# Cached attention decode with a squared-ReLU gate: the start and the end of the work sent through the loop's value product

## The chip, the core and the metric

The kernel runs on one core of a Trainium2 chip. TensorE (PE) multiplies, VectorE (DVE), ScalarE (ACT) and GpSimd (POOL) do the work between products, SyncE (SP) issues the transfers (DMAs) from the memory of the chip into the core's SBUF. Sixteen DMA engines carry them. The metric is the time of one execution on the device in microseconds (us), median of several runs.

## What is computed

```python
xn = layernorm(x)                                  # x: 2 x 1 x 512
q = (xn @ wq) -> 2 x 32 heads x 1 x 128            # wq: 512 x 4096
p = softmax(q . k_cache * 128 ** -0.5)             # k_cache: 2 x 8 x 32768 x 128, four q heads share one
o = p . v_cache                                    # v_cache: 2 x 8 x 32768 x 128
s = o @ wo                                         # wo: 4096 x 512
h = relu(xn @ w1 + b1) ** 2                        # w1: 512 x 1792
out = x + s * silu(h @ w2 + b2)                    # w2: 1792 x 512
```

All is float32. The two caches are 537 MB of the 561 MB that are read.

## The kernel before, in words

**Streams and steps.** The caches are 16 streams (8 key-value heads, 2 batch rows), each cut into two halves, so the loop has 32 steps. A step needs one block of keys (8 MB, tile `kslot`) and one of values (8 MB, tile `vslot`), of which there is one buffer each. The step's scores are 32 products into `sc` (L319). VectorE takes their maximum (L265), a transpose through TensorE and a second reduction make it one per head (L269, L273), ScalarE takes the exponential (L278), TensorE turns the result (L325), ScalarE copies it to `pT` (L280). Then 32 products of 16 x 512 multiply `pT` with `vslot` into `o_ps` (L305): this is the **value product**. ScalarE copies `o_ps` (L228), TensorE turns it (`ot`, L310), VectorE sums its blocks (L243), and once in two steps GpSimd weighs the two halves into `oT` (L248 to L252).

**What sets the order.** TensorE's program is a loop of two blocks, `pe_values` and `pe_scores`, that waits on semaphores against a counter; its start and its end are two more blocks, `pe_first` and `pe_last`, recorded by the class `Later`. The other engines' programs are written out for all 32 steps. SP's queue is in program order: the gate's weights `wm` (into `wbuf`), `wq` (into `vslot`), the first keys; then for each step the values as soon as the value product before has left `vslot` (wait at L255), and the next keys as soon as the scores have left `kslot` (L259); at the end, with no wait of their own, `wo` in six pieces of 16, 8, 4, 2, 1 and 1 heads into `wbuf` (L335), which has been free since the gate. All of these share one queue, so a transfer starts when those issued ahead of it are through.

**Start.** ScalarE's queue loads x, b1 and b2 as small rows. The layernorm (L147 to L173) runs on all 128 partitions with two small products of `ones`. The gate is computed by products of its own into the PSUM tile `wb`: 16 for w1 (L185), 14 for w2 (L200), 4 to gather them (L206). In round 0 of the loop the value product multiplies xn (spread over `pT` at L177) with `wq` in `vslot`: this gives q.

**End.** After the last value product and its weighing, `pe_last` multiplies the heads of `oT` with `wo` as the pieces come: 28 heads into `wb` (L348), the last 4 and the gathered sum of the 28 into `acc` (L354, L359). Then VectorE multiplies with the gate and adds x (L370, L372), and the output goes out (L374).

Of the kernel before, what the change touches and what calls it, by code (L numbers as in the profile page):

```python
# [22 lines left out]
FG = F // NG  # L23
FJ = FG // 32
# [3 lines left out]
PIECES = (16, 8, 4, 2, 1, 1)  # L28
WIDE = 28
SCALE = 1.0 / math.sqrt(DH)  # L30
# [20 lines left out]
class Later:  # L51


    def __init__(self, engine):
        self.engine, self.calls = engine, []

    def __call__(self, f, *a, **k):
        self.calls.append([f, a, k, False])

    def wait(self, *tokens):  # L60
        for token in tokens:
            self(self.engine.wait, token)

    def done(self):
        self.calls[-1][3] = True
        self.engine.n += 1
        return self.engine.sem, self.engine.n

    def emit(self):
        self.engine.seen = {}  # L70
        for f, a, k, last in self.calls:
            ins = f(*a, **k)  # L72
            if last:
                ins.then_inc(self.engine.sem, 1)


def build(nc, x32, x16, kt, vt, wq, wm, wo, out):
# [3 lines left out]
    PE = [mybir.EngineType.PE]  # L81
# [39 lines left out]
    t_one = pool.done(g.memset(ones[:, :], 1.0))  # L121
    t_xT = pool.done(g.memset(xT[:, :], 0.0))
    g.memset(selq[:, :], 0.0)
    t_pT = pool.done(g.memset(pT[:, :], 0.0))
    t_qz = pool.done(g.memset(qz[:, :], 0.0))
    t_oT = pool.done(g.memset(oT[:, :, :], 0.0))
    t_o0 = dve.done(nc.vector.memset(o_ps[:, :], 0.0))

    act.wait(t_xb)
    for lo, hi in ((0, 15), (15, 28), (28, 32)):  # L130
        nc.scalar.dma_start(small[lo:hi, :], x32[lo:hi]).then_inc(small_sem, 16)
    for lo, hi in ((0, 14), (14, 16)):
# [7 lines left out]
    v.tensor_reduce(selg[:, :], ident[:, :].rearrange("p (g y) -> p y g", g=NG), axis=AX.X, op=ALU.add)  # L140
    dve.wait(t_qz)
    t_sel = dve.done(v.tensor_reduce(selq[:, 0:32:16], ident[:, :].rearrange("p (g y) -> p y g", g=NG)[:, 0:2], axis=AX.X, op=ALU.add))


    first = Later(pe)
    first.wait(t_id, (small_sem, 48))
    first(tr, ms[:, 0:32], small[0:32, :], ident[0:32, 0:32])  # L147
    dve.wait(first.done())
    t = dve.done(v.tensor_copy(xs[:, :], ms[:, 0:22]))
    first.wait(t, t_one)  # L150
    first(mm, ms[:, 32:40], ones[:, :], xs[:, 0:8], start=True, stop=True)
    dve.wait(first.done())
    t = dve.done(v.tensor_reduce(st[:, 0:2], ms[:, 32:40].rearrange("p (d b) -> p b d", b=B), axis=AX.X, op=ALU.add))
    dve.wait(t)
    t = dve.done(v.tensor_scalar(st[:, 2:4], st[:, 0:2], -1.0 / D, None, op0=ALU.mult))
    dve.wait(t)
    t = dve.done(v.tensor_tensor(xc[:, :].rearrange("p (d b) -> p d b", b=B), xs[:, 0:8].rearrange("p (d b) -> p d b", b=B),
                                 st[:, None, 2:4].to_broadcast([P, ND, B]), op=ALU.add))
    dve.wait(t)
    t = dve.done(v.tensor_mul(sq[:, :], xc[:, :], xc[:, :]))  # L160
    first.wait(t)
    first(mm, ms[:, 64:72], ones[:, :], sq[:, :], start=True, stop=True)
    dve.wait(first.done())
    t = dve.done(v.tensor_reduce(st[:, 4:6], ms[:, 64:72].rearrange("p (d b) -> p b d", b=B), axis=AX.X, op=ALU.add))
    dve.wait(t)
    t = dve.done(v.tensor_scalar(st[:, 6:8], st[:, 4:6], 1.0 / D, 1e-5, op0=ALU.mult, op1=ALU.add))
    act.wait(t)
    t = act.done(nc.scalar.activation(st[:, 8:10], st[:, 6:8], AF.Sqrt))
    dve.wait(t)
    t = dve.done(v.reciprocal(st[:, 10:12], st[:, 8:10]))  # L170
    dve.wait(t, t_xT)
    t_x = dve.done(v.tensor_tensor(xT[:, :, 0:B], xc[:, :].rearrange("p (d b) -> p d b", b=B),
                                   st[:, None, 10:12].to_broadcast([P, ND, B]), op=ALU.mult))  # L173
    dve.wait(t_x, t_pT)
    pq = pT[:, :].rearrange("p (d f y h) -> p d f y h", d=ND, f=2, h=REP)
    for f in range(2):
        ins = v.tensor_copy(pq[:, :, f, :, 2 * f:2 * f + 2], xT[:, :, None, 0:B].to_broadcast([P, ND, 16, B]))  # L177
    ins.then_inc(gv, 1)


    first.wait(t_x, (wm_sem, 16))
    for d in range(ND):
        for c in range(NG):
            lo = d * F + c * FG
            first(mm, wb[32 * c:32 * c + 32, :FG], xT[:, d, :], wbuf[:, lo:lo + FG], start=(d == 0), stop=(d == ND - 1))  # L185
    dve.wait(first.done())
    t = dve.done(v.tensor_copy(o_sb[:, :FG], wb[:, :FG]))
    dve.wait(t)
    t = dve.done(v.transpose(hT[:, :, :].rearrange("p j b -> p (j b)"), o_sb[:, :FG]))
    dve.wait(t)  # L190
    t = dve.done(v.tensor_tensor(hT[:, :, 0:B], hT[:, :, 0:B], xs[:, 8:22, None].to_broadcast([P, FJ, B]), op=ALU.add))
    dve.wait(t)
    t = dve.done(v.tensor_scalar(hT[:, :, 0:B], hT[:, :, 0:B], 0.0, None, op0=ALU.max))
    dve.wait(t)
    t = dve.done(v.tensor_mul(hT[:, :, 0:B], hT[:, :, 0:B], hT[:, :, 0:B]))
    first.wait(t)
    for j in range(FJ):
# [24 lines left out]
    q_token = [None]
    t_rl = t_add = t_dx = t_wl = t_wr = None
    t_t4 = {}
    for i in range(NT + 1):
        s, u = divmod(i, 2)
        act.wait(at(VD, i))
        nc.scalar.copy(o_sb[:, :], o_ps[:, :]).then_inc(os, 1)  # L228
        if i and not u:

            dve.wait(t_lt)
            t_rl = dve.done(v.reciprocal(rl[:, :], lt[:, :]))
        dve.wait(at(OT, i))
# [19 lines left out]
        if i == NT:  # L253
            break
# [11 lines left out]
        if t_dx and not u:  # L266
            dve.wait(t_dx)
# [151 lines left out]
```

## Time and profile before

| | |
|---|---|
| time, median of 3 runs | 1303.61 us (1303.28 to 1303.71) |
| the profiled execution's own time | 1303.31 us |
| its span, from the first to the last instruction | 1302.0 us |
| TensorE busy | 53% |
| DMA queue of SP | 561.06 MB, 99.7% of 16 engines' span |
| granted TensorE clock, mean | 0.739 |

How to read it: the span is what the rows describe, and the time of an execution is 1.31 us more than its span. A DMA row gives the time from issue to landing, so it includes the time spent behind earlier transfers. A row of the timeline gives start, duration, engine, line, operation, the number of instructions merged, and in brackets how long the engine had been idle and for whom. "PE ... x64" is one value product: a float32 product is two instructions.

### The profile page before, as it was taken

How to read it: one execution, taken by the hardware profiler on the slowest of the kernel's cores; microseconds unless marked ns; L12 is line 12 of the kernel's file. 1: busy time of each engine (PE TensorE's matmuls, PEld its weight loads, DVE VectorE, ACT ScalarE, POOL GpSimd, SP SyncE). 2: the span in 40 equal slices, each digit the busy share in tenths (PEclk: the TensorE clock that was granted, in tenths of full speed). 3: DMA queues.
4: the chain of work that ended last, by engine and by line, in shares of the span. 5: the costliest groups of instructions: out<-in, count | busy, mean ns of one | idle time of the engine just before them, and what ended most of it. 6: DMA issues, size and time to landing. Idle time of an engine off the chain costs nothing.

```text
span 1302.0 us, 10280 instructions
## 1 busy us (share of the span) xinstructions
PE 690.4 (53%) x4685; PEld 191.6 (15%) x4685; DVE 54.2 (4%) x186; ACT 72.3 (6%) x184; POOL 34.9 (3%) x174
## 2 busy tenths in 40 slices
PE   3446446546546545645645654644654554554556
PEld 1111111111111111111111111111111111111111
DVE  1000000000000000000000000000000000000000
ACT  0100000000000000000000000000000000000000
POOL 0000000000000000000000000000000000000000
PEclk9777677677677768667767767767767867777778
DMA  9999999999999999999999999999999999999998
GB/s 418 421 449 421 449 421 445 423 445 425 429 441 421 447 423 445 425 441 429 439 429 427 443 421 447 423 445 425 443 427 439 429 439 431 421 447 423 443 427 357
DMA packets 10617, 561.18 MB, mean 431 GB/s; under 512 B 1216, under 2 KB 1392, under 8 KB 1776
## 3 DMA queue, kind: packets, MB, share of 16 engines
q1 hardware_dynamic: 10512, 561.06, 99.7%
q8 instruction: 2, 0.03, 0.0%
q14 instruction: 7, 0.06, 0.0%
q10 hardware_dynamic: 96, 0.03, 0.0%
HBM read 561.02 MB, written 0.07 MB: 431 GB/s over the span
## 4 chain that ended last, share of the span: by engine, by line
DMA 76%; PE 23%; issue 0%; SPq 0%; DVE 0%
DMA vslot<-in_vt 70%; PE o_ps L305 23%; DMA wbuf<-in_wo 4%; DMA vslot<-in_wq 3%; PE acc L72 0%; SPq L335 0%; SPq L104 0%; SPq L256 0%; DVE yb L370 0%; DVE xb L372 0%; SPq L105 0%
## 5 line engine op out<-in xcount | busy, mean ns | idle before, releaser
L319 PE MATMUL sc<-kslot,qz 128*32 128x512 f32 x2048 | 298.9, 749 | 277.8 <-DMA kslot<-in_kt 277.8
L305 PE MATMUL o_ps<-vslot,pT 128*16 128x512 f32 x2112 | 307.2, 747 | 203.7 <-DMA vslot<-in_vt 196.5
L319 PEld LDWEIGHTS sc<-kslot,qz 128*32 128x32 f32 x2048 | 72.1, 134 | 483.1 <-DMA kslot<-in_kt 285.4
L305 PEld LDWEIGHTS o_ps<-vslot,pT 128*16 128x16 f32 x2112 | 64.4, 114 | 419.2 <-issue 212.4
L278 ACT ACTIVATE prob<-sc,nm 128x512 f32<-128x512 f32 x32 | 22.0, 687 | 661.7 <-DVE nm L273 661.7
L325 PE MATMUL tp<-ident,prob 128*128 128x128 f32 x128 | 28.3, 360 | 53.5 <-ACT prob L278 53.5
L228 ACT COPY o_sb<-o_ps 128x512 f32<-128x512 f32 x33 | 19.3, 586 | 494.1 <-PE o_ps L305 494.1
L265 DVE TENSOR_REDUCE r<-sc 128x1 f32<-128x512 f32 x32 | 22.1, 692 | 570.7 <-PE sc L319 570.7
L310 PE MATMUL ot<-ident,o_sb 128*128 128x128 f32 x132 | 21.7, 287 | 23.6 <-ACT o_sb L228 23.6
L243 DVE TENSOR_REDUCE t<-ot 128x4 f32<-128x64 f32 x32 | 7.2, 225 | 547.7 <-PE ot L310 547.7
L263 POOL COPY qz<-qT 128x4 f32<-128x4 f32 x31 | 5.8, 188 | 833.3 <-PE sc L319 833.3
L325 PEld LDWEIGHTS tp<-ident,prob 128*128 128x128 f32 x128 | 18.1, 178 | 59.6 <-ACT prob L278 59.6
L322 PE MATMUL ms<-ident,r 128*128 128x128 f32 x32 | 10.3, 323 | 26.4 <-DVE r L265 26.4
L310 PEld LDWEIGHTS ot<-ident,o_sb 128*128 128x128 f32 x132 | 13.9, 141 | 54.0 <-ACT o_sb L228 54.0
L280 ACT COPY pT<-tp 128x512 f32<-128x512 f32 x32 | 18.8, 586 | 31.2 <-PE tp L325 31.2
L327 PEld LDWEIGHTS ms<-selh,l 128*128 128x128 f32 x64 | 13.6, 263 | 0.0
L322 PEld LDWEIGHTS ms<-ident,r 128*128 128x128 f32 x32 | 4.2, 133 | 55.4 <-DVE r L265 55.4
L327 PE MATMUL ms<-selh,l 128*128 128x4 f32 x64 | 11.4, 248 | 0.0
L72 PE MATMUL ms<-ident,small 32*128 32x32 f32 x1 | 0.3, 283 | 18.2 <-DMA small<-in_x 18.2
L269 DVE TENSOR_REDUCE mh<-ms 128x4 f32<-128x128 f32 x32 | 9.3, 292 | 13.3 <-PE ms L322 13.3
L250 POOL TENSOR_TENSOR tw<-t,wr 128x8 f32<-128x8 f32 x16 | 3.2, 203 | 247.9 <-DVE t L243 247.9
L271 POOL TENSOR_TENSOR mm<-mh,selm 128x4 f32<-128x4 f32 x32 | 6.5, 203 | 77.1 <-DVE mh L269 77.1
(74 smaller groups left out, 82.0 us busy)
## 6 DMA issues: line engine op xcount, KB each, us to landing
wbuf<-in_wm SPq DMA_DIRECT2D x1, 7168.0 KB, 20.7
wbuf<-in_wo SPq DMA_DIRECT2D x1, 4096.0 KB, 39.3
wbuf<-in_wo SPq DMA_DIRECT2D x1, 2048.0 KB, 43.7
wbuf<-in_wo SPq DMA_DIRECT2D x1, 1024.0 KB, 46.1
kslot<-in_kt SPq DMA_DIRECT2D x32, 29.2
vslot<-in_vt SPq DMA_DIRECT2D x32, 29.3
wbuf<-in_wo SPq DMA_DIRECT2D x1, 512.0 KB, 46.8
wbuf<-in_wo SPq DMA_DIRECT2D x2, 256.0 KB, 47.1
```

The lines of the kernel that those rows point to most:

```text
L228: nc.scalar.copy(o_sb[:, :], o_ps[:, :]).then_inc(os, 1)
L243: t_t4 = dve.done(v.tensor_reduce(t4[:, 1 - u, :], ot[:, :].rearrange("p (i y e) -> p e i y", i=4, y=NG)[:, :REP], axis=AX.XY, op=ALU.add))
L265: v.tensor_reduce(r1[:, :], sc[:, :], axis=AX.X, op=ALU.max).then_inc(dm, 1)
L269: t_mh = dve.done(v.tensor_reduce(mh[:, u, :], ms[:, :P].rearrange("p (a h) -> p h a", h=REP), axis=AX.X, op=ALU.max))
L278: nc.scalar.activation(prob[:, :], sc[:, :], AF.Exp, bias=nm[:, u:u + 1], scale=SCALE, accum_out=l1[:, :]).then_inc(ex, 1)
L280: nc.scalar.copy(pT[:, :], tp[:, :]).then_inc(gv, 1)
L305: ins = mm(o_ps[32 * y:32 * y + 16, :], pT[:, 16 * n:16 * n + 16], vslot[:, n * W:(n + 1) * W], start=(n < NG), stop=(n >= 32 - NG))
L310: ins = tr(ot[:, lo:lo + P], o_sb[:, n * DH:(n + 1) * DH], ident[:, :])
L319: ins = mm(sc[32 * c:32 * c + 32, :], qz[:, 28 - 4 * j:60 - 4 * j], kslot[:, lo:lo + W], start=(j == 0), stop=(j == NJ - 1))
L322: tr(ms[:, :P], r1[:, :].to_broadcast([P, P]), ident[:, :]).then_inc(pe.sem, 1)
L325: ins = tr(tp[:, k * P:(k + 1) * P], prob[:, k * P:(k + 1) * P], ident[:, :])
L327: mm(ms[:, :REP], l1[:, :].to_broadcast([P, P]), selh[:, :], start=True, stop=True).then_inc(pe.sem, 1)
```

## The change

- **Gate through the value product.** `wm` goes into `vslot`, packed on the host to blocks of 512 columns, w1 in blocks 0 to 15 with two of w2's at 11 and 15, the rest of w2 in blocks 16 to 27. `wq` goes into `wbuf`. PE has no blocks of its own for the start: `pe_values` runs three rounds (`PRO = 3`) before the first scores. Round 0 multiplies xn with w1, round 1 the squared ReLU with w2 (both read `vslot` as it is). Then ACT, POOL and DVE copy `wq` from `wbuf` to `vslot` (5700, 5884 and 4800 columns of each partition), and round 2 gives q. The first values are issued after round 2.
- **Layernorm** on two partitions of 512 elements, VectorE alone, with x, b1 and b2 in one load of 8 rows (`xr`), issued after POOL's first instruction; a 32 x 32 transpose and four copies lay the rows out over the partitions (`xs`).
- **End through the value product.** The last values come in two halves on two semaphores (`gv`, `gb`). A value product now waits at blocks 16, 24 and 28 too (`gb`, `gc`, `gd`), and counts `vh` after block 15. When the last values' first half is multiplied, SP issues 12 heads of `wo` into that half of `vslot`; when the second half is, 8, 4 and 4 heads more, then the last 4 heads one by one into `wbuf`. A 36th round multiplies the 28 heads in `vslot` with `pT` (filled from `oS`, L379); the last 4 heads and the gathering are as before.
- **Loops.** VectorE's and ScalarE's programs are loops of 16 rounds (one stream each) with waits against registers; what POOL did in the steps (the key queries `qz`, the maximum's scaling, the weighing) is VectorE's. `Later` and PSUM tile `wb` go.

The diff's core (the host's packing, declarations and the waits of VectorE's loop, which repeat, left out):

```diff
-PIECES = (16, 8, 4, 2, 1, 1)
+PRO = 3
+PIECES = (12, 8, 4, 4)
+TAIL = (1, 1, 1, 1)
...
-    nc.sync.dma_start(wbuf[:, 0:2 * FJ * D], wm).then_inc(wm_sem, 16)
-    nc.sync.dma_start(vslot[:, :], wq).then_inc(gv, 16)
+    nc.sync.dma_start(vslot[:, 0:WM], wm).then_inc(gv, 16)
+    nc.sync.dma_start(wbuf[:, :], wq).then_inc(wq_sem, 16)
     nc.sync.dma_start(kslot[:, :], kt[0, 0]).then_inc(gs, 16)
...
+    o_copy(pro(VD, 0))
+    pool.wait(pro(VD, 0))
+    t_z = pool.done(g.memset(pT[:, :], 0.0))
+    dve.wait(pro(OT, 0))
...
+    for lo, hi, at in ((0, 2, slice(11, 16, 4)), (2, NF, slice(16, 28))):
+        ins = v.tensor_copy(hT[:, at, :, 0:B], hv[:, lo:hi, None, :].to_broadcast([P, hi - lo, 4, B]))
+    ins.then_inc(gv, 17)
+
+    o_copy(pro(VD, 1))
+    pool.wait(pro(VD, 1))
+    t_z = pool.done(g.memset(pT[:, :], 0.0))
+    cuts = (0, 4800, 10500, SLOT)
+    act.wait((wq_sem, 16))
+    t_c0 = act.done(nc.scalar.copy(vslot[:, cuts[1]:cuts[2]], wbuf[:, cuts[1]:cuts[2]]))
+    pool.wait((wq_sem, 16))
+    t_c1 = pool.done(g.tensor_copy(vslot[:, cuts[2]:cuts[3]], wbuf[:, cuts[2]:cuts[3]]))
+    dve.wait(pro(VD, 1), (wq_sem, 16))
+    t_c2 = dve.done(v.tensor_copy(vslot[:, cuts[0]:cuts[1]], wbuf[:, cuts[0]:cuts[1]]))
...
+    dve.wait(t_c0, t_c1, t_c2, t_f)
+    v.tensor_copy(st[:, 6:7], selh[:, 0:1]).then_inc(gv, 17)
...
+    sp.wait(pro(VD, 2))
+    nc.sync.dma_start(vslot[:, :], vt[0, 0]).then_inc(gv, 16)
...
+    with nc.body("sp_last", valid_engines=SP):
+        sp.wait((vh, NT + PRO))
+        h = 0
+        for n, sem in zip(PIECES, (gv, gb, gc, gd)):
+            if h:
+                sp.wait(at(VD, NT - 1))
+            nc.sync.dma_start(vslot[:, (TOP + h) * D:(TOP + h + n) * D], wo[h * P:(h + n) * P].rearrange("(p h) e -> p (h e)", h=n)).then_inc(sem, 16)
+            h += n
+        for n, sem in zip(TAIL, tail_sem):
+            nc.sync.dma_start(wbuf[:, (h - WIDE) * D:(h - WIDE + n) * D], wo[h * P:(h + n) * P].rearrange("(p h) e -> p (h e)", h=n)).then_inc(sem, 16)
...
+    with nc.body("pe_values", valid_engines=PE):
+        i = nc.snap(it, min_val=0, max_val=NT + PRO)
+        w(gv, i * 17 + 17)
+        for n in range(32):
+            if n in (16, 24, 28):
+                w({16: gb, 24: gc, 28: gd}[n], i * 16 + 1)
             y = n % NG
             ins = mm(o_ps[32 * y:32 * y + 16, :], pT[:, 16 * n:16 * n + 16], vslot[:, n * W:(n + 1) * W], start=(n < NG), stop=(n >= 32 - NG))
+            if n == 15:
+                ins.then_inc(vh, 1)
         ins.then_inc(pe.sem, 1)
+        nc.br_lt(it, NT + PRO, on_true="pe_turn", on_false="end", engines=PE)
```

SP's queue at the end, in the kernel before, from the last keys on (`vt` are the values, `kt` the keys; a name in brackets is what the instruction waits for):

```order
L260 DMA kslot<-in_kt 128x16384 [waits pe]
L256 DMA vslot<-in_vt 128x16384 [waits pe]
L335 DMA wbuf<-in_wo 128x8192
L335 DMA wbuf<-in_wo 128x4096
L335 DMA wbuf<-in_wo 128x2048
L335 DMA wbuf<-in_wo 128x1024
L335 DMA wbuf<-in_wo 128x512 x2
```

and in the change:

```order
L237 DMA kslot<-in_kt 128x16384 [waits pe]
L242 DMA vslot<-in_vt 128x8192 [waits pe]
L243 DMA vslot<-in_vt 128x8192
L244 UNCONDITIONAL_BRANCH
L325 DMA vslot<-in_wo 128x6144 [waits vh]
L325 DMA vslot<-in_wo 128x4096 [waits pe]
L325 DMA vslot<-in_wo 128x2048 x2
L328 DMA wbuf<-in_wo 128x512 x4
```

Before, all of `wo` stands behind the last values without a wait; now two waits on TensorE stand between the last values and `wo`.

VectorE's queue in the change between the gate's second product and the first keys' query (in the kernel before `wq` lands in `vslot` itself and nothing stands here but the gate's own steps):

```order
L201 COPY vslot<-wbuf 128x4800 [waits wq,pe]
L203 TENSOR_REDUCE y<-ot 128x8 [waits pe]
L207 COPY pT<-xs 128x4x16x2 [waits pool]
L207 COPY pT<-xs 128x4x16x2
L209 TENSOR_TENSOR y<-y,xs 128x8 [waits dve]
L211 COPY st<-selh 128x1 [waits pool,dve,act]
L223 COPY qT<-ot 128x4x4x2 [waits pe]
```

The copy at L211 is the one that lets TensorE start round 2: it waits for the three copies of `wq`.

## Rows read from the trace of the kernel before

**Rows 1.** The page: SP's DMA queue (packets, MB, share), and the chain.
```profile
q1 hardware_dynamic: 10512, 561.06, 99.7%
...
DMA vslot<-in_vt 70%; PE o_ps L305 23%; DMA wbuf<-in_wo 4%; DMA vslot<-in_wq 3%; PE acc L72 0%; SPq L335 0%; SPq L104 0%; SPq L256 0%; DVE yb L370 0%; DVE xb L372 0%; SPq L105 0%
```

**Rows 2.** Timeline of the start (start us, duration us, engine, what, idle before).
```profile
18.17 0.28 PE L72 MATMUL ms<-ident,small 32*128 32x32 f32 x1 [18.17 <-DMA small<-in_x]
...
28.87 3.63 PE L72 MATMUL wb<-wbuf,hT 128*32 128x512 f32 x28 [2.10 <-DVE hT L195]
...
40.82 9.50 PE L305 MATMUL o_ps<-vslot,pT 128*16 128x512 f32 x64 [7.22 <-DMA vslot<-in_wq]
...
50.40 0.33 SPq L256 DMA_DIRECT2D vslot<-in_vt  x1
50.41 0.59 ACT L228 COPY o_sb<-o_ps 128x512 f32<-128x512 f32 x1 [15.66 <-PE o_ps L305]
...
51.74 0.31 DVE L237 COPY qT<-ot 128x32 f32<-128x32 f32 x2 [16.67 <-PE ot L310]
...
60.17 8.38 PE L319 MATMUL sc<-kslot,qz 128*32 128x512 f32 x64 [8.47 <-DMA kslot<-in_kt]
```

**Rows 3.** The chain in order of time: the first values' transfer, the fastest and the slowest product.
```profile
50.40 29.08 DMA vslot<-in_vt
...
118.23 8.41 PE o_ps L305 x64
...
234.34 10.08 PE o_ps L305 x64
```

**Rows 4.** DMA issues: KB each, us from issue to landing.
```profile
wbuf<-in_wm SPq DMA_DIRECT2D x1, 7168.0 KB, 20.7
...
wbuf<-in_wo SPq DMA_DIRECT2D x2, 256.0 KB, 47.1
out<-xb SPq DMA_DIRECT2D x1, 64.0 KB, 1.5
```

**Rows 5.** DMA queues, packets between 6 and 9.5 us (packets, MB, share).
```profile
q10 hardware_dynamic: 29, 0.01, 0.9%
```

**Rows 6.** Groups of instructions, shapes apart (count, busy us, mean ns).
```profile
L284 ACT COPY lh<-ms 128x4 f32<-128x4 f32 x32 | 5.4, 168 | 0.0
L187 DVE COPY o_sb<-wb 128x448 f32<-128x448 f32 x1 | 0.6, 625 | 4.6 <-PE wb L72 4.6
L126 POOL MEMSET oT<- 128x1024 f32 x1 | 1.0, 954 | 0.0
L124 POOL MEMSET pT<- 128x512 f32 x1 | 0.5, 528 | 0.0
L177 DVE COPY pT<-xT 128x128 f32<-128x128 f32 x2 | 0.4, 224 | 0.0
L155 DVE TENSOR_SCALAR st<-st 128x2 f32<-128x2 f32 x1 | 0.2, 169 | 0.0
```

**Rows 7.** Waits: who waited for whom, us in total, times, longest.
```profile
DVE r L265 <- PE sc L319: 570.7, 32, 18.4
```

**Rows 8.** Timeline of the end.
```profile
1249.70 2.80 SPq L335 DMA_DIRECT2D wbuf<-in_wo  x6
...
1272.69 0.59 ACT L280 COPY pT<-tp 128x512 f32<-128x512 f32 x1 [0.74 <-PE tp L325]
...
1279.29 9.79 PE L305 MATMUL o_ps<-vslot,pT 128*16 128x512 f32 x64 [6.52 <-DMA vslot<-in_vt]
...
1291.14 0.20 POOL L252 TENSOR_TENSOR oT<-tw 128x4 f32<-128x4 f32 x1
...
1299.27 0.43 PE L72 MATMUL acc<-wbuf,oT 128*32 128x128 f32 x8
```

**Rows 9.** Two stretches near the end (length, busy of each engine, granted clock, DMA).
```profile
1264.40:1274.60 10.20, 5.88 (x55) 1.91 (x44) 1.39 (x5) 1.54 (x5) 1.01 (x5) 1.00 0.95 411
1274.60:1284.80 10.20, 5.51 (x28) 1.18 (x32) 0.00 (x0) 0.00 (x0) 0.00 (x0) 0.50 1.01 437
```

More of the change, by code (lines that the diff above doesn't have):

```diff
@@ L22 @@
 HALF = SK // 2
[L23 to L24 removed]
+NF = F // P
 SLOT = HALF
@@ L48, in done, with build @@
         return self.sem, self.n
[L51 to L77, printed above, removed]
+def build(nc, xr, x16, kt, vt, wq, wm, wo, out):
     pe, act, dve, pool, sp = (Engine(nc, e, n) for e, n in (
@@ L149, in build @@
[L149 to L153, printed above, removed]
+    dve.wait(t_sg)
+    v.tensor_reduce(selg[:, 0:32:16], ident[:, :].rearrange("p (g y) -> p y g", g=NG)[:, 0:2], axis=AX.X, op=ALU.add).then_inc(ex, PRO)
+    dve.wait((xr_sem, 16))
+    t = dve.done(v.tensor_reduce(st[0:B, 0:1], xin[0:B, :], axis=AX.X, op=ALU.add))
@@ L159, in build @@
     dve.wait(t)
[L160 to L164, printed above, removed]
+    t = dve.done(v.tensor_mul(xsq[0:B, :], xin[0:B, :], xin[0:B, :]))
     dve.wait(t)
-    t = dve.done(v.tensor_scalar(st[:, 6:8], st[:, 4:6], 1.0 / D, 1e-5, op0=ALU.mult, op1=ALU.add))
+    t = dve.done(v.tensor_reduce(st[0:B, 2:3], xsq[0:B, :], axis=AX.X, op=ALU.add))
@@ L175, in build @@
+    t = dve.done(v.tensor_reduce(y8[:, :, :], ot[:, :].rearrange("p (i y e) -> p i e y", i=4, y=NG)[:, :, 0:B, :], axis=AX.X, op=ALU.add))
+    dve.wait(t_z)
     pq = pT[:, :].rearrange("p (d f y h) -> p d f y h", d=ND, f=2, h=REP)
     for f in range(2):
[L177 to L185, printed above, removed]
@@ L300, in build @@
[L300 to L312 removed]
+        t_f = dve.done(v.tensor_copy(pq[:, :, f, :, 2 * f:2 * f + 2], xs[:, :, None, 0:B].to_broadcast([P, ND, 16, B])))
@@ L340, in build @@
[L340 to L352 removed]
+        nc.br("pe_values", engines=PE)
@@ new lines, in build @@
+    act.wait((pe.sem, 2 * PRO + 6 * NT + 1))
+    t_w = [act.done(nc.scalar.copy(o_sb[:, k:k + D // 2], o_ps[:, k:k + D // 2])) for k in (0, D // 2)]
+    pe.n = at(OT, NT - 1)[1] + 1
+    pe.wait(t_gp)
+    t = pe.done(tr(ms[:, :P], gpad[:, :], ident[:, :]))
+    dve.wait(t)
+    t_gate = dve.done(v.tensor_copy(gate[:, :], ms[:, :P]))
+    wv = wbuf[:, 0:TOP * D].rearrange("p (h e) -> p h e", e=D)
+    h = 0
+    pe.wait(t_add)
+    for n, sem in zip(TAIL, tail_sem):
+        pe.wait((sem, 16))
+        for h in range(h, h + n):
@@ L360, in build @@
         h += 1
-    t_acc = last.done()
-    with nc.body("pe_last", valid_engines=PE):
-        last.emit()
-        nc.br("end", engines=PE)
-    with nc.body("pe_first", valid_engines=PE):
-        first.emit()
-        nc.tensor.br_lt(it, NT, on_true="pe_values", on_false="end").branch_hint(hint)
-    nc.switch_bb("end")
-    dve.wait(t_acc, t_gate)
+    t = pe.done(ins)
+    dve.wait(t, t_gate)
     t = dve.done(v.tensor_mul(yb[:, :], gate[:, :], acc[:, :P]))
-    dve.wait(t, (xb_sem, 32))
```

419 lines of the change are left out of this document (221 added, 198 removed).

## The prediction, made blind

> **What bounds the kernel now.** I read the page first, then the chain, then the timeline of both ends. The page's queue row says it: SP's DMA queue is busy for 99.7% of the span, and the chain alternates between the values' transfer and the value product that frees `vslot` [rows 1]. So the kernel is a stream of 561 MB with something ahead and something behind it, and a change of the engines' work costs or gains only where the queue runs dry, or where it lies ahead of the first or behind the last byte. In the timeline of the start the reader is to see two landings: `wq` at 40.8 us (the product that waits for it starts at 40.82) and the first keys at 60.13 (the scores start at 60.17, 0.04 after their landing), and between them the issue of the first values at 50.40 [rows 2]. That is 9.7 us ahead of the keys' landing; the values land 29.08 us after issue, at 79.48, so 8 MB take 79.48 - 60.13 = 19.35 us, and the queue never waits [rows 3]. In the rows of the loop the value product takes 8.41 to 10.08 us [rows 3], by how much of it falls on the clock's lower level, against 19.35 us for the block in flight beside it: some 9 us of reserve in every step.
>
> **How late an issue may be.** A transfer of 64 KB with nothing ahead of it lands 1.5 us after its issue [rows 4]. I take that as the fixed part: an issue costs nothing if it stands 1.5 us ahead of the landing of the transfer before it, and every us later is a us of the kernel. For the first values the limit is 60.13 - 1.5 = 58.6 us.
>
> **The start, step by step.** `wm` has the same bytes, first in the queue: it lands at 0.72 + 20.7 = 21.4 us [rows 4]. Ahead of it the layernorm must be done. Of the small packets 29 have run by 9.5 us [rows 5], and `xr` needs 16 (8 rows and their 8 closings) and is issued earlier than those: I take 9.5 us. Five wide VectorE steps of 512 elements at 0.63 us or a little more (the copy of 448), ten short ones and ScalarE's root at 0.17 to 0.22 us [rows 6], with the gaps: 6.5 us. That ends at 16, 5 us ahead of `wm`. Were the rows as late as the small loads before (18.2 us [rows 2]), it would be 24.7 and everything below 3.3 us later.
>
> Round 0: 21.4 + 9.5 (the product after an idle stretch [rows 2]) = 30.9. ScalarE's copy and TensorE's turn lie between 50.41 and 51.74 before [rows 2]: 1.35, so 32.3. Six short VectorE steps, 0.2 each and gaps: 33.6. Round 1 comes 1.4 us after TensorE's last work. The gate's second product came 2.1 us after, and its 28 instructions took 3.63 us [rows 2], 0.43 for four: the upper level. So 64 take 7.0 to 7.5, and round 1 ends at 41; at 10.08 [rows 3] it would be 43.7. `wq` is there at 40.8, so the copies start at about 41.2.
>
> ScalarE: its own copy of `o_ps` first (0.59), then 5700 columns at (586 - 168) / 508 = 0.82 ns each, from the copies of 512 [rows 2] and of 4 columns [rows 6]: 4.9 us, done at 46.8. VectorE: from PSUM (625 - 169) / 446 = 1.02 ns a column, but the copy of 128 between SBUF tiles took 224, so (224 - 169) / 126 = 0.44 [rows 6]: 4800 columns take 2.3 to 5.1 us, done at 46.3 at the latest; 0.9 us of short steps follow. POOL: a memset first (0.53), then 5884 columns. The trace has no wide copy of POOL's. The nearest rows are memsets, (954 - 528) / 512 = 0.83 ns a column [rows 6]: 4.9 us, done at 46.7. A copy also reads, and if that takes as long again, 9.8 us, done at 51.6. I take 4.9, because that row is nearest, and keep 9.8. So round 2 starts at 47.2, behind an idle TensorE: 9.6, and the values are issued at **56.9**, 1.7 us inside the limit. Hole at the start: **0**, covered by the first keys' transfer; the cover ends at 58.6.
>
> [...]
>
> **The loops.** VectorE takes POOL's seven short steps (0.17 each by its own short ones [rows 6]) and branches; the longest chain, scores to `pT`, may grow by about a us. TensorE gets three waits more in a product. VectorE waits 570.7 / 32 = 17.8 us in each step for scores [rows 7], and the values' product had to wait 6.5 us for its values even in the last step [rows 8]. What hides all this is that reserve; I cost it at 0. Gone, it would be 1 to 2 us in 32 steps, 30 to 60 us, but 9 us of reserve do not go.
>
> **The end, step by step.** Before, `wo` stands behind the last values without a wait; the last values land at 1279.25, the last piece of `wo` at about 1252.1 + 47.1 = 1299.2, where the last product starts [rows 4, 8], and 2.8 us follow to the end of the span. Now `wo`'s first 12 heads wait for the first half of the last product. Its values land 9.7 us earlier, at 1269.6, but `pT` is only ready at 1272.69 + 0.59 = 1273.3 [rows 8]. Half a product is 3.5 us at the upper level and 6.9 at the lower. The clock was at the upper level until 1274.6 and at the lower after it [rows 9], with TensorE idle; now TensorE works there. So 1276.8 to 1280.2 against a limit of 1279.25 - 1.5 = 1277.7: a hole of 0 to 2.5 us. I take **1.0**, nearer to the lower end, because the upper level holds when it starts. The second half starts at 1279.3 and ends at 1282.8 to 1286.2; 12 of 32 heads take 19.35 x 12 / 32 = 7.26 us, so its limit is 1279.25 + 1.0 + 7.26 - 1.5 = 1286.0: **0**, at most 0.2 more. From the product's end to the weighed heads it took 2.3 us before (1289.08 to 1291.34 [rows 8]), and filling `pT` adds 0.5, so round 35 starts near 1287, with the first piece, and needs 7 to 10 us: it follows the pieces, the last of which (4 heads) lands about 3 us ahead of the stream's end. The last 4 heads and what follows are as before: **0**.
>
> **Bytes.** None go; `wm` is padded to the same size, and the caches and `wo` stay. Nothing in the sum is negative. Ahead of the first DMA nothing moves.
>
> **Sum.** Against the profiled execution's 1303.31: 0 (start) + 0 (loops) + 1.0 (end) = 1304.3. That execution is 0.3 below the median of the runs, so I predict **1304.6 us**, which is no change: a measurement here tells 0.2%, 2.6 us, from nothing, so 1301.0 to 1306.2 count as the same.
>
> **Rivals.**
> *POOL's copy is slow* (the other side: slower). If it takes 9.8 us, round 2 starts at 51.9, the values are issued at 61.5, and the queue is empty for 2.9 us: 1307.5. From 6.6 us for that copy on it decides. For it: POOL must read and write each column. Against it: only that the trace has no sign of it. Chance 0.20.
> *The copies exclude each other.* VectorE goes first at 41.2 for 2.3 us, POOL's memset and copy follow and end at 48.9: round 2 starts at 49.3, the values are issued at 58.9, a hole of 0.3. With POOL first VectorE's copy ends at 49.0 and its short steps at 49.9: a hole of 1.1. That is 1304.9 to 1305.7; with round 1 at its slow end 2.5 us more. Chance 0.22, of which 0.17 inside the bound of no change. With the slow copy as well it is 1309.9.
> *The way out of VectorE's loop is slow.* Before, no program but TensorE's branches. If VectorE has to fetch what stands behind its loop from memory while the queue is full, as the small loads that took until 18.2 us [rows 2], then `pT` comes some 15 us late and round 35 with it; it has 1 to 2 us of reserve: up to 1317. [...] Chance 0.04.
> *Nothing runs dry at all.* The hole at the end is 0: 1303.6. To be faster by over 0.2% the stream would need fewer bytes. Chance of that 0.03; that nothing changes at all lies in the forecast.
>
> **How the numbers follow.** The forecast (0 at the start, 0 to 2.5 at the end) has 0.51 and gives 1303.6 to 1306.1. With 0.17 of the second rival, and 0.01 of the third for a short fetch, the same has 0.69; slower has 0.20 (slow copy) + 0.05 + 0.03 = 0.28, faster 0.03. The range goes from 1302.8, a little under the forecast's lower end for the scatter of a profile, to 1309.0, which takes in the slow copy alone but not with the exclusion or the fetch.
>
> **What would show it.** Right: SP's queue share stays at 99.5% or more; the first values are issued between 56 and 58.6 us and land at 79.5; the loop's rounds repeat at 38.7 us; the first piece of `wo` is issued near 1278, and the last landing is 19.9 to 21.5 us behind the last values. Wrong at the start: the first values land later than 80, and POOL's copy takes over 6.6 us or starts behind VectorE's. Wrong at the end: `wo`'s first piece is issued after 1280, or round 35 ends more than 2 us after the fourth piece's landing. Wrong as a whole: a loop round longer than 38.8 us.

## The result, and the profile after

| | before | after |
|---|---|---|
| median | 1303.49 us (1303.28 to 1303.71, 12 runs) | 1306.14 us (1304.68 to 1308.25, 12 runs) |
| ratio, 95% interval | | 1.0022 (1.0014 to 1.0031) |
| profiled execution | 1303.31 | 1308.21, span 1306.8 |

The change costs 2.65 us, on the edge of what the prediction called no change (2.6 us). The forecast was 1304.6; the interval of the ratio is 1.8 to 4.0 us. The runs after lie 3.6 us apart, those before 0.4, and the profiled execution after is one of the longer: its rows show the loss in full size, the median some half of it.

The page's queue row, which answers to the first of [rows 1] (99.7%):

```profile
q1 hardware_dynamic: 10944, 561.06, 99.4%
```

0.3% of 1306.8 us is 3.9 us: the queue now runs dry. Where, the two ends say. First the timeline of the start, after (start us, duration us, engine, what, idle before):

```profile
20.65 8.75 PE L357 MATMUL o_ps<-vslot,pT 128*16 128x512 f32 x64 [20.65 <-DMA vslot<-in_wm]
...
31.85 7.06 PE L357 MATMUL o_ps<-vslot,pT 128*16 128x512 f32 x64 [1.09 <-DVE pT L189]
...
39.98 4.94 ACT L197 COPY vslot<-wbuf 128x5700 f32<-128x5700 f32 x1 [0.42 <-DMA wbuf<-in_wq]
...
40.02 5.09 POOL L199 COPY vslot<-wbuf 128x5884 f32<-128x5884 f32 x1 [0.49 <-DMA wbuf<-in_wq]
...
40.05 7.56 DVE L201 COPY vslot<-wbuf 128x4800 f32<-128x4800 f32 x1 [8.26 <-DMA wbuf<-in_wq]
...
56.95 0.33 SPq L227 DMA_DIRECT2D vslot<-in_vt  x1
...
59.36 7.07 PE L340 MATMUL sc<-kslot,qz 128*32 128x512 f32 x64 [1.10 <-DVE qz L225]
...
80.01 9.78 PE L357 MATMUL o_ps<-vslot,pT 128*16 128x512 f32 x64 [10.08 <-DMA vslot<-in_vt]
```

The reader should see three things. All three copies start within 0.07 us, as `wq` lands; GpSimd's takes 5.09 us, and VectorE's ends 2.50 us after it. The first values are issued at 56.95. And the first scores no longer wait for the keys but for the query (`qz`). By `wq`'s landing at 39.96 and 19.35 us for a block, the keys were there at about 59.3, so the values should have been multiplied from 78.7 on; they were at 80.01.

What the queue moved shows the same. Windows of the two kernels, before and then after (length, busy of PE, PEld, DVE, ACT, POOL with counts, granted clock, DMA share, GB/s):

```profile
57.00:60.00 3.00, 0.00 (x0) 0.00 (x0) 0.00 (x0) 0.00 (x0) 0.00 (x0) 0.50 0.86 371
60.00:80.00 20.00, 9.96 (x75) 3.08 (x79) 1.14 (x3) 1.43 (x4) 0.39 (x2) 0.76 1.04 452
```

```profile
57.00:60.00 3.00, 1.30 (x12) 0.70 (x16) 0.48 (x3) 1.83 (x2) 0.00 (x0) 1.00 1.01 350
60.00:80.00 20.00, 7.53 (x67) 2.51 (x59) 1.38 (x5) 1.43 (x4) 0.00 (x0) 0.80 0.97 419
...
1274.60:1284.80 10.20, 9.73 (x67) 2.14 (x65) 0.68 (x4) 0.76 (x3) 0.00 (x0) 0.73 0.63 243
```

Between 57 and 80 us the stream moved 10.15 MB before and 9.43 MB after. The last row stands against the second of [rows 9]: 243 GB/s where it was 437, in the stretch between the last values and `wo`.

The timeline of the end, after, which answers to [rows 8], and the first piece of `wo` from the page's DMA issues (KB, us to landing):

```profile
1274.70 0.59 ACT L306 COPY pT<-tp 128x512 f32<-128x512 f32 x1 [1.21 <-PE tp L346]
...
1275.34 9.45 PE L357 MATMUL o_ps<-vslot,pT 128*16 128x512 f32 x64 [0.46 <-ACT pT L306]
...
1281.42 4.76 SPq L325 DMA_DIRECT2D vslot<-in_wo  x4
...
1286.98 0.20 DVE L379 COPY pT<-oS 128x64 f32<-128x64 f32 x1
...
1291.64 8.97 PE L357 MATMUL o_ps<-vslot,pT 128*16 128x512 f32 x56 [5.47 <-DMA vslot<-in_wo]
...
1305.25 0.35 SPq L409 DMA_DIRECT2D out<-xb  x1
```

```profile
vslot<-in_wo SPq DMA_DIRECT2D x1, 3072.0 KB, 10.2
```

`pT` is ready at 1275.3, half the last value product takes 6.06 us (1275.34 to the wake of SP near 1281.4), and `wo`'s first piece lands 10.2 us after its issue. TensorE, whose `pT` for round 35 is filled at 1287.2, then waits for that piece until 1291.64.

The loop, before and after, by two scores that waited for their keys, 26 pairs of blocks apart:

```profile
253.70 8.90 PE L319 MATMUL sc<-kslot,qz 128*32 128x512 f32 x64 [7.96 <-DMA kslot<-in_kt]
...
1259.94 9.24 PE L319 MATMUL sc<-kslot,qz 128*32 128x512 f32 x64 [9.31 <-DMA kslot<-in_kt]
```

```profile
254.81 9.44 PE L340 MATMUL sc<-kslot,qz 128*32 128x512 f32 x64 [9.12 <-DMA kslot<-in_kt]
...
1261.04 9.78 PE L340 MATMUL sc<-kslot,qz 128*32 128x512 f32 x64 [8.77 <-DMA kslot<-in_kt]
```

1006.24 us before, 1006.23 after. Against the kernel before, the profiled execution after lost 1.1 us by the 254th microsecond, nothing in the next thousand, and from the last scores to the issue of `out` it needs 1305.25 - 1261.04 = 44.21 us where it took 1300.40 - 1259.94 = 40.46: 3.75 more. These two numbers, the start's and the end's, are what I read from every run below.

### The profile page after: what moved, and what is told of

Same layout as the page of the kernel before. It is cut to its first block, busy times and chain, and to the rows that moved or that the text cites. A ratio compares the mean times of both kernels' runs of the same rounds, so it can differ in the third digit from the quotient of the medians.

```text
span 1306.8 us, 11116 instructions
## 1 busy us (share of the span) xinstructions
PE 697.6 (53%) x4757; PEld 191.6 (15%) x4757; DVE 88.1 (7%) x360; ACT 97.0 (7%) x202; POOL 10.7 (1%) x22
## 3 DMA queue, kind: packets, MB, share of 16 engines
q1 hardware_dynamic: 10944, 561.06, 99.4%
## 4 chain that ended last, share of the span: by engine, by line
DMA 74%; PE 24%; DVE 1%; issue 0%; SPq 0%; ACT 0%; DVEq 0%
DMA kslot<-in_kt 70%; PE sc L340 23%; DMA wbuf<-in_wq 3%; PE o_ps L357 1%; DMA wbuf<-in_wo 1%; DVE vslot L201 1%; SPq L325 0%; PE tp L346 0%; SPq L328 0%; PE acc L397 0%; DVE r L269 0%; DVE qz L225 0%; PE ot L367 0%; ACT pT L306 0%; ACT o_sb L172 0%
## 5 line engine op out<-in xcount | busy, mean ns | idle before, releaser
L357 PE MATMUL o_ps<-vslot,pT 128*16 128x512 f32 x2304 | 333.8, 744 | 235.9 <-DMA vslot<-in_vt 199.3
L357 PEld LDWEIGHTS o_ps<-vslot,pT 128*16 128x16 f32 x2304 | 70.1, 114 | 470.0 <-issue 229.0
L269 DVE TENSOR_REDUCE r<-sc 128x1 f32<-128x512 f32 x32 | 22.1, 692 | 550.9 <-PE sc L340 550.9
L304 ACT ACT_TABLE_LOAD x16 | 20.5, 1283 | 0.3
L348 PEld LDWEIGHTS ms<-selh,l 128*128 128x128 f32 x64 | 13.1, 254 | 0.0
L201 DVE COPY vslot<-wbuf 128x4800 f32<-128x4800 f32 x1 | 7.6, 7559 | 8.3 <-DMA wbuf<-in_wq 8.3
L304 ACT ACTIVATION_READ_ACCUMULATOR prob<-sc,nm 128x1 f32 x32 | 6.2, 193 | 0.0
L308 ACT COPY lh<-ms 128x4 f32<-128x4 f32 x32 | 5.4, 168 | 0.0
## 6 DMA issues: line engine op xcount, KB each, us to landing
vslot<-in_wm SPq DMA_DIRECT2D x1, 7168.0 KB, 19.9
vslot<-in_wo SPq DMA_DIRECT2D x1, 3072.0 KB, 10.2
```

The source lines that it names most:

```text
L201: t_c2 = dve.done(v.tensor_copy(vslot[:, cuts[0]:cuts[1]], wbuf[:, cuts[0]:cuts[1]]))
L269: v.tensor_reduce(r1[:, :], sc[:, :], axis=AX.X, op=ALU.max).then_inc(dm, 1)
L304: nc.scalar.activation(prob[:, :], sc[:, :], AF.Exp, bias=nm[:, u:u + 1], scale=SCALE, accum_out=l1[:, :]).then_inc(ex, 1)
L348: mm(ms[:, :REP], l1[:, :].to_broadcast([P, P]), selh[:, :], start=True, stop=True).then_inc(pe.sem, 1)
L357: ins = mm(o_ps[32 * y:32 * y + 16, :], pT[:, 16 * n:16 * n + 16], vslot[:, n * W:(n + 1) * W], start=(n < NG), stop=(n >= 32 - NG))
```

## The experiments

The theories: **A**, the queue is empty at the end, because `wo` waits for half of the last value product. **B**, it is empty at the start, because the first values wait for the copies of `wq`. **C**, the loops cost something. **D** came with the first three runs: code that stands far enough behind the head of TensorE's program comes late. That the copies of `wq` slow the stream itself is ruled out: from 40 to 58 us the queue moved 408 GB/s in the kernel after and 408 in e2 (below), which has no copies.

All profiles in one table: the start of the value product near 234 us, the last scores' start, the stretch from there to `out`, each from the timeline; differences are to the kernel before.

| kernel | median (runs' range) | ratio, 95% interval | value product near 234 | end's stretch |
|---|---|---|---|---|
| before | 1303.49 (1303.28 to 1303.71) | | 234.34 | 40.46 |
| after | 1306.14 (1304.68 to 1308.25) | 1.0022 (1.0014, 1.0031) | 235.45, +1.11 | 44.21, +3.75 |
| e1 `wo` behind the values | 1307.84 (1307.16 to 1308.32) | 1.0032 (1.0020, 1.0045) | 236.64, +2.30 | 42.93, +2.47 |
| e2 q from `wbuf` | 1309.05 (1307.43 to 1309.75) | 1.0042 (1.0028, 1.0055) | 233.91, -0.43 | 46.18, +5.72 |
| e3 both | 1304.66 (1304.07 to 1306.01) | 1.0013 (1.0003, 1.0022) | 233.98, -0.36 | 42.18, +1.72 |
| e4 TensorE kept busy | 1305.81 (1304.53 to 1307.00) | 1.0016 (1.0007, 1.0025) | 235.09, +0.75 | 42.27, +1.81 |
| e5 is e1, shifted | 1306.33 (1304.93 to 1307.92) | 1.0020 (1.0011, 1.0029) | 238.50, +4.16 | 40.37, -0.09 |
| e6 is e2, shifted | 1304.69 (1303.76 to 1307.75) | 1.0014 (1.0005, 1.0023) | 234.19, -0.15 | 44.07, +3.61 |
| e7 is e3, shifted | 1303.31 (1302.97 to 1304.82) | 1.0002 (0.9993, 1.0011) | 234.19, -0.15 | 40.36, -0.10 |
| e8 no GpSimd copy | 1306.36 (1303.99 to 1309.01) | 1.0023 (1.0013, 1.0032) | 234.98, +0.64 | 42.02, +1.56 |

The fourth column understates the start's loss, because its zero lies late. In the kernel before, e6 and e7 a packet of 16 KB runs on an instruction queue (q8 in the page's DMA queues) in the first 15 us, and `wm` lands 20.5 to 20.7 us after its issue; in the others none runs there, and it lands after 19.6 to 20.1. That the packet delays the stream fits and was not tried. e2 has no such packet and no hole at the start, so 233.91 is the better zero: against it the kernel after lost 1.54 us, e4 1.18, e8 1.07, e1 2.73.

**e1: all of `wo` into `wbuf`, behind the last values without a wait.** The last product of 28 heads is written out behind the loop and reads `wbuf`.

```diff
+    for n, sem in zip(PIECES, piece_sem):
+        nc.sync.dma_start(wbuf[:, (TOP + h) * D:(TOP + h + n) * D], wo[h * P:(h + n) * P].rearrange("(p h) e -> p (h e)", h=n)).then_inc(sem, 16)
...
-    with nc.body("sp_last", valid_engines=SP):
-        sp.wait((vh, NT + PRO))
...
+    for n, sem in zip(PIECES, piece_sem):
+        pe.wait((sem, 16))
+        for h in range(h, h + n):
+            y, k = h % NG, TOP + h
+            ins = mm(o_ps[32 * y:32 * y + 16, :], pT[:, 16 * k:16 * k + 16], wbuf[:, k * W:(k + 1) * W], start=(h < NG), stop=(h >= WIDE - NG))
```

> The change with its end undone: all 32 heads of wo go into wbuf, issued right behind the last values without a wait; the last product of 28 heads is written out behind the loop. Theory A (the queue runs dry at the end, because wo's first piece waits for half of the last value product): no hole at the end, the last landing 19.8 to 20.2 us behind the last values, 1304.0 to 1304.7 us, and the runs lie within 0.6 us of each other. Theory B (the loss is at the start, where the first values wait for the copies of wq): 1305.5 to 1306.2, runs as far apart as the change's 3.6 us. Theory C (the loops of VectorE and ScalarE cost something in each step): 1306.

Measured: slower than the change. The timeline of e1 explains it, by the copies at the start and TensorE at the end:

```profile
41.59 3.06 DVE L199 COPY vslot<-wbuf 128x4800 f32<-128x4800 f32 x1 [8.88 <-PE o_ps L347]
...
42.09 7.51 POOL L197 COPY vslot<-wbuf 128x5884 f32<-128x5884 f32 x1
...
44.67 5.14 DVE L205 COPY pT<-xs 128x128 f32<-128x128 f32 x2
...
1303.64 0.30 PE L394 MATMUL acc<-wbuf,oN 128*32 128x128 f32 x2 [1.41 <-issue]
```

Here round 1 ended later (8.76 us for the product instead of 7.06), so VectorE was first: now its copy is short and GpSimd's ends 4.95 us after it; VectorE's next two small copies, 0.35 us together in the kernel after, take 5.14 and end 0.2 us after GpSimd's. At the end TensorE stands still for 1.41 us and no semaphore is named. So e1 could not decide on A: it brought two losses of its own.

**e2: round 2 reads `wq` from `wbuf`; no copies.** The values are issued after round 1; the end is the change's.

```diff
-    t_c0 = act.done(nc.scalar.copy(vslot[:, cuts[1]:cuts[2]], wbuf[:, cuts[1]:cuts[2]]))
-    t_c1 = pool.done(g.tensor_copy(vslot[:, cuts[2]:cuts[3]], wbuf[:, cuts[2]:cuts[3]]))
-    t_c2 = dve.done(v.tensor_copy(vslot[:, cuts[0]:cuts[1]], wbuf[:, cuts[0]:cuts[1]]))
...
-    sp.wait(pro(VD, 2))
+    sp.wait(pro(VD, 1))
...
+    with nc.body("pe_q", valid_engines=PE):
+        w(wq_sem, 16)
...
+            ins = mm(o_ps[32 * y:32 * y + 16, :], pT[:, 16 * n:16 * n + 16], wbuf[:, n * W:(n + 1) * W], start=(n < NG), stop=(n >= 32 - NG))
```

> The change with the copies of wq taken away: the third round multiplies with wbuf where wq landed, and the first values are issued after the second round, at about 39 us. The end is the change's. Theory A: only the small loss of the start goes, 1305.0 to 1305.8, and the runs still lie 3 us apart. Theory B: 1303.3 to 1303.8. Theory C: 1306.

Measured: the start's loss is gone (233.91), which is B, yet the median is 2.9 us above the change's, outside all three forecasts. Its end holds the same sort of stop as e1's, among the same last products (timeline of e2):

```profile
1303.97 0.53 PE L402 MATMUL acc<-wbuf,oN 128*32 128x128 f32 x11 [2.49 <-issue]
```

**e3: both edits at once.**

> Both edits together: wq read where it landed, wo without a wait; the loops stay. Theories A and B: the stream never runs dry, 1303.0 to 1303.8, same as before, runs within 0.6 us. Theory C: 1304.5 or more.

Measured: neither hole is left, and still 1.2 us over the kernel before, which by itself is theory C's forecast. The stop is now in the middle of the last product (timeline of e3):

```profile
1292.53 7.03 PE L383 MATMUL o_ps<-wbuf,pT 128*16 128x512 f32 x44 [2.80 <-issue]
```

e1 and e2 make TensorE's program longer by one product each, e3 by two, and the stop moves forward by as much: in all three it lies some 215 product records behind the head of the program. The program of the kernel after has some 180 and shows no such row. That is theory D.

A transfer runs at each stop. The pages' DMA queues list an instruction queue, q8, here in e1 and then in e3 (packets, MB, share):

```profile
q8 instruction: 1, 0.02, 0.0%
```

```profile
q8 instruction: 2, 0.03, 0.0%
```

By the packet records of the traces, one packet of 16 KB starts at 1301.27 us in e1, at 1301.59 in e2 and at 1289.96 in e3. That is at the stop each time (it begins at 1302.23, 1301.48 and 1289.73), and TensorE goes on 1.44 to 1.51 us after the packet's end. e3's second packet, at 1296.26, passes without a stop. The pages of the kernel after, e4 and e8 have no row q8, and none of them has the stop. That the packet holds TensorE's code is my reading of the queue's name; no view tells what is in it.

**e4: TensorE kept busy.** The kernel after, with 3, 6 and 3 products of 128 columns whose results nobody uses, in its waits between the scores and `pT`. It adds work and asks whether the length of the hole at the end hangs on the clock.

```diff
+        for _ in range(6):
+            mm(acc[:, :P], ident[:, :], ident[:, :], start=True, stop=True)
         w(ex, i + 1)
```

> The change with 12 products of 128 columns (identity by identity, result unused) put into TensorE's waits between the scores and the copy to pT, so that TensorE is busy there. If the hole at the end is as long as it is because the last value product's first half falls on the clock's lower level, it now runs at the upper one more often: wo's first piece is issued 1.5 to 3 us earlier against the last values' landing, 1304.6 to 1305.4, runs nearer together. If the level does not follow from what TensorE did just before, 1306.1 to 1306.8, because the added products delay pT a little.

Measured (timeline of e4, the last value product in its two halves and the issue of `wo`):

```profile
1273.58 3.63 PE L363 MATMUL o_ps<-vslot,pT 128*16 128x512 f32 x32
...
1277.27 9.51 SPq L325 DMA_DIRECT2D vslot<-in_wo  x4
...
1280.10 5.32 PE L363 MATMUL o_ps<-vslot,pT 128*16 128x512 f32 x32 [2.90 <-DMA vslot<-in_vt]
```

The first half took 3.63 us, about half of the 7.06 that a whole product takes at a granted clock of 1.00 (round 1 of the kernel after), where the kernel after had 6.06 at 0.60; `wo` went out 2.8 us ahead of the last values' landing at 1280.1, and the end's loss fell from 3.75 to 1.81 us. The rest came later: the second half took 5.32 us (the granted clock was 0.83 from 1274.6 to 1284.8). The median gained 0.3 us, less than the intervals tell apart, and lies in neither of the two ranges expected.

**e5, e6, e7: the same three, with TensorE's program shifted.** Waits that are met at once stand at its head, and in e6 and e7 `pe_q` is written ahead of the loop, so that the place of the stop falls elsewhere.

```diff
+    for _ in range(388):
+        w(pool.sem, 1)
     nc.br("pe_values", engines=PE)
```

That is e5; e6 and e7 have 128 (the expectations count half as many instructions, 194 and 64).

> The first experiment again (wo in wbuf, no wait) with 194 wait instructions that are met at once at the head of TensorE's program, which move all of its code by that many places. In the first and second experiment TensorE stood still for 1.4 and 2.5 us for nothing that the trace shows, each at the same distance (some 215 products) from the head of its program. Theory D (the program's code behind a certain place comes late, and there TensorE waits): no such stand at the end, 2 to 2.6 us less than the first experiment, 1304.5 to 1306.0 us. If the stand has another cause it stays with the same products, 1307 to 1308.3. Theory A expects further that the last landing is 20 us behind the last values, so that what is left over the kernel before (1.0 to 2.5 us) is the start's.

> The second experiment again (wq read from wbuf, no copies, the change's own end), the third round's code moved ahead of the loop and 64 met waits at the head, so that the loop and the end lie together. Theory D: 2 to 2.6 us less than the second experiment, 1305 to 1307. Theory A: the end's hole of 2 to 3.7 us is all that is left over the kernel before, runs 2 us or more apart. Theory B: 1303.5.

> The third experiment again (both edits) with the same move of the code. Theories A, B and D together: no hole at the start, none at the end, no stand of TensorE behind the last values: 1302.7 to 1303.6 us, the runs within 0.6 us, at or below the kernel before. Theory C (the loops cost something): 1304.3 or more.

Measured: the stops at the end are gone in all three (the end's stretch is 2.56, 2.11 and 1.82 us shorter than in e1, e2 and e3), and their instruction packet now runs at the start, at 26.7 us in e5, in the middle of a product, and at 13.1 in e6 and e7, while TensorE waits for `wm`; no stop goes with it there. This is what D expected of the place; how the packet and the stop hang together is not shown. The medians of e5 and e6 lie just outside D's ranges, 0.3 us above and 0.3 below. In e7's profiled execution nothing is left of any loss (timeline of e7, then what answers to the 19.35 us of [rows 3]: 79.38 - 60.04 = 19.34):

```profile
60.04 8.62 PE L333 MATMUL sc<-kslot,qz 128*32 128x512 f32 x64 [9.60 <-DMA kslot<-in_kt]
...
79.38 9.17 PE L350 MATMUL o_ps<-vslot,pT 128*16 128x512 f32 x64 [7.22 <-DMA vslot<-in_vt]
...
1300.12 0.35 SPq L411 DMA_DIRECT2D out<-xb  x1
```

e7 has the change's loops, its gate in the value product and its way out of VectorE's loop, and its median is that of the kernel before: C falls, and the loss is in the two holes. One thing is left open: e7's runs lie 1.9 us apart, where 0.6 was expected, and four of the eleven take 1304.2 to 1304.8 us; the one profiled is among the fastest. e6 has the end's hole alone (+3.61 in the profiled execution, +1.2 in the median), e5 the start's alone, but not at its own size, since the many waits at the head made the first product late (timeline of e5; 20.65 in the kernel after):

```profile
22.84 1.91 PE L349 MATMUL o_ps<-vslot,pT 128*16 128x512 f32 x8 [22.84 <-issue]
```

So e5 is a dose of B: the first values are issued at 61.34, 2.5 us later than in e1 and after the keys' landing, and the product near 234 is 4.16 us late instead of 2.30.

**e8: no GpSimd in the copies.**

```diff
-    cuts = (0, 4800, 10500, SLOT)
+    cuts = (0, 9000, SLOT)
...
-    t_c1 = pool.done(g.tensor_copy(vslot[:, cuts[2]:cuts[3]], wbuf[:, cuts[2]:cuts[3]]))
```

> The changed kernel, with wq copied by VectorE (9000 columns) and ScalarE (7384) alone; GpSimd copies nothing. The end stays as in the change, so its hole stays too. Theory B with the exclusion (VectorE's 7.56 us in the change are 5.09 of waiting for GpSimd and 2.47 of work, 0.51 ns a column): VectorE takes about 4.6 us, ScalarE about 6.4 and ends last, near 46.4 us; the third round starts about 1.2 us earlier than 48.3, the first values are issued near 55.7 (56.95 in the change), the first value product starts 19.35 us behind the keys' landing, near 78.5 (80.01 in the change), and the sixth one near 234.1 (235.45), as in the kernel before (234.34). Median about 1 us under the change's, 1305.1. If VectorE is slow by itself (7.56 us of its own work for 4800 columns): 14 us, the values go out at 64, the first value product starts near 86, median near 1312. If the start's loss has nothing to do with the values' issue: 235.4 as in the change, and the same median, 1306.1.

Measured (timeline of e8, start and end):

```profile
39.76 6.34 ACT L197 COPY vslot<-wbuf 128x7384 f32<-128x7384 f32 x1
...
39.83 4.85 DVE L199 COPY vslot<-wbuf 128x9000 f32<-128x9000 f32 x1 [7.91 <-DMA wbuf<-in_wq]
...
44.70 0.35 DVE L205 COPY pT<-xs 128x128 f32<-128x128 f32 x2
...
56.22 0.33 SPq L225 DMA_DIRECT2D vslot<-in_vt  x1
...
79.80 8.41 PE L355 MATMUL o_ps<-vslot,pT 128*16 128x512 f32 x64 [8.63 <-DMA vslot<-in_vt]
...
1273.18 5.32 PE L355 MATMUL o_ps<-vslot,pT 128*16 128x512 f32 x32 [0.55 <-ACT pT L304]
...
1278.56 6.43 SPq L323 DMA_DIRECT2D vslot<-in_wo  x4
```

VectorE moves 9000 columns in less time than 4800 beside GpSimd (4.85 against 7.56 us), 0.54 ns a column, and its small copies are back at 0.35. So the exclusion is shown in both orders: VectorE behind GpSimd in the kernel after (7.56 us, of which 2.59 are work at e8's rate), GpSimd behind VectorE in e1 (7.51 us for the 5.09 of the kernel after). But the forecast of the time missed. Round 2 started 1.9 us earlier and took 9.74 us instead of 8.56, so the values went out only 0.7 us earlier, and their product started 0.2 us earlier, not 1.5. The median is not below the change's. Dropping GpSimd from the copies is not enough; the issue at about 40 us, in e6 and e7, was.

## Why the prediction was right, and where its working failed

The time lay inside the range, 1.5 us above the forecast, and the kind of loss was the one predicted: the stream is the bound, no byte went, and what counts is whether the queue runs dry. That it lay inside is in part luck. The forecast's own branch (0 at the start, 0 to 2.5 at the end) reached 1306.1; the rest of the range, up to 1309.0, was held open for a slow copy of GpSimd, which did not come, and took in holes of another cause. By the prediction's own signs the end was wrong: `wo`'s first piece was issued after 1280, at 1281.42, the last landing came 23.7 us behind the last values (1304.07 against 1280.40) and not 19.9 to 21.5. The queue's share was 99.4%, just under its 99.5 for right, and the first values landed at 79.97, between its 79.5 for right and its 80 for wrong. Point by point:

**The start's clock was right, its limit was not.** Round 0 was to end at 30.9 and ended at 29.4, round 1 at 41 and ended at 39; the values were to be issued at 56.9 and were at 56.95. That is partly luck, since the copies took longer than the step had it (to 47.6 instead of 46.7) and began earlier. `wm` landed 0.8 us earlier than counted, and so did the keys (59.31 instead of 60.13), so by its own rule the limit was 57.8 and the issue still inside it. What failed is the step "I take that as the fixed part": 1.5 us, from a transfer of 64 KB [rows 4]. What an issue needs ahead of it is the time from issue to landing less 19.35 us for the bytes, and in the runs with a hole that was 2.5 to 4.2 us:

| kernel | issue ahead of the keys' landing, us | hole behind the keys, us |
|---|---|---|
| e7 (e2, e3 and e6 likewise) | 19.9 | 0 |
| before [rows 2] | 9.7 | 0 |
| e8 | 2.9 | 1.3 |
| after | 2.4 | 1.3 |
| e4 | 1.9 | 0.6 |
| e1 | 0.3 | 2.2 |
| e5 | -1.3 | 3.9 |

(A landing is the last of a transfer's sixteen semaphore counts in the trace; a minus is an issue behind it.) A later issue does not always cost more: e4's is later than that of e8 and of the kernel after, and it lost less. By the packet records the values' first packet of 64 KB takes up to 3.5 us in these runs, where later ones take 2.42. In the kernel after two of the first sixteen packets start at 59.28 and 59.54, 0.7 us and more behind the rest, and the landing waits for the last; in e4 all sixteen have started by 59.10. Why single ones start late is not shown, and where between 2.9 and 9.7 us the loss ends was not tried. So the hole forecast as 0 was 1.5 us, by 235.45 against 233.91 in e2, which differs at the start alone (1.3 by the landings).

**The exclusion came true, its price did not.** The rival "the copies exclude each other" had GpSimd first, VectorE done at 49.0 and a hole of 1.1 us. That two such copies exclude each other was an assumption, which no row of the kernel before shows, and its 0.22 my estimate. The runs of the change show it. In the kernel after GpSimd was first by 0.03 us, and VectorE's 4800 columns took 7.56 us, its 5.09 and 2.47 more (0.51 ns a column, against 0.54 in e8); in e1 VectorE was first by 0.50, and GpSimd's 5884 columns took 7.51 us and ended 4.95 after VectorE's. GpSimd's copy, 5884 columns in 5.09 us, was 0.87 ns a column: the memset's rate was the right row, and the rival of a slow copy fell. The rival's loss, though, was to come from the later issue alone, and the issue was inside the limit; e8, without the exclusion, lost as much behind the keys.

**The loops: 0, and right.** The waits of VectorE for scores are 550.9 us in 32 steps after (570.7 before, [rows 7]), so 17 us of reserve a step stayed.

```profile
DVE r L269 <- PE sc L340: 550.9, 32, 18.4
```

That is the waits view of the kernel after. The way out of VectorE's loop was not slow either. No run shows VectorE waiting for a fetch of its program, the third rival's case, long or short (0.01 of its chance); what the kernel after shows is `pT` filled 2.4 us after the last value product's end (1284.79 to 1287.18), and 2.8 had been counted.

**The end: the right place, the wrong size.** The term 1.0 us (0 to 2.5) was 3.75 in the profiled execution. Three parts of its working: `pT` was to be ready at 1273.3 and was at 1275.3, because the stream was 1.1 us late by the start's hole and the last scores and the transposes ran more at the lower level (9.78 us at a granted clock of 0.72 against 9.24 at 0.76, and 1.12 at 0.50 against 0.66 at 1.00). Half the product took 6.06 us of the 3.5 to 6.9 allowed; I took the lower end's side "because the upper level holds when it starts", and it did not: the granted clock was 0.60 of full speed while that half ran. From 1270.9 to 1275.3 TensorE had worked 1.7 of 4.4 us, and the clock was at 0.5 when the half began. And the fixed part was 1.5 again: `wo`'s first piece, 12 of 32 heads or 7.26 us of bytes, landed 10.2 us after its issue, which makes 2.9. The first half's time and the loss at the end go together in part: 5.32 us with 1.56 (e8), 5.9 with 3.61 (e6), 6.06 with 3.75. e4 has 3.63 us and yet 1.81, most of it from the later pieces and not from the first hole. That this is what spreads the runs (3.6 us after, 0.4 before) is not borne out: e5, whose `wo` waits for no product, has runs 3.0 us apart, and e3 and e7 1.9. What spreads them stays open.

**The sum.** Of the median's 2.65 us, e6 gives 1.45 to the start (1306.14 to 1304.69) and e7 another 1.38 to the end (1304.69 to 1303.31), each known to about 1 us; e6 and e7 also have the shifted program. The forecast's 0 + 1.0 was wrong at both ends in the same direction, by one shared term, the time that a queue needs to run again (1.5 us taken; 2.5 to 4.2 at the start and 2.9 at the end measured), and at the end also by the lower clock in the first half (0.60).

No version here beats the kernel before; e7 equals it. The stream of 561 MB is the same in all.

## What to carry to other kernels

Where a kernel is one long stream of transfers, keep the queue's next block issued many microseconds ahead of the end of the block before it, not the 1.5 us of one short transfer ahead: here issues 1.9 to 2.9 us ahead still lost 0.6 to 1.3 us, and one 9.7 us ahead lost nothing. Compute put between two blocks, at the ends as in the loop, has to be priced at the slower clock level (6.06 us for half a product here at a granted clock of 0.60, where e4 had 3.63), and work that reads a spare buffer (e7) leaves the issue free of it. When an experiment is slower than every theory allows, look for a stop that no semaphore explains before giving up the theory: three runs here carried one of 1.4 to 2.8 us, and the instruction queue among the DMA queues is where to look.

## What had not been expected of the hardware

A copy of VectorE between SBUF tiles and one of GpSimd did not go on side by side: with GpSimd first (the kernel after) VectorE's takes 7.56 us and ends 2.50 after GpSimd's, with VectorE first (e1) GpSimd's takes 7.51 instead of 5.09, and even VectorE's two copies of 128 columns then take 5.14 instead of 0.35. Without GpSimd's (e8) VectorE moves 9000 columns in 4.85 us.

TensorE stops for 1.41, 2.49 and 2.80 us without a semaphore to wait for, at one distance from the head of its program (e1 to e3), and no longer when the program is shifted (e5 to e7). A packet of 16 KB on the instruction queue q8 runs at each of the stops, and at the start where the program is shifted. A full queue is not the reason. In e1 no other packet ran between 1301 and 1304 us, where TensorE stopped; in e5 the packet at 26.7 ran beside a full queue, and TensorE did not stop. What decides it is not shown.

An 8 MB transfer that was issued 2.9 us ahead of the landing before it, or later, needed 21.9 to 23.6 us from issue to use (the kernel after, e1, e4, e5 and e8); issued 9.7 us ahead in the kernel before and 19.9 in e7, the same transfer was there 19.35 and 19.34 us behind the one before it.
